# A retention layer and a gated feed-forward in one kernel: the later blocks' loads in a new order, and two small copies on another queue

## The chip, the cores and the metric

The kernel runs on one core of a Trainium2 chip. The metric is the device time of one execution in microseconds (us). The kernel before took 308.02 us (median of three runs, 307.03 to 310.31).

## The reference, cut to what matters

Eight sequences of 576 positions with eight heads of 64 features go through a retention layer: scores between a query and all earlier keys, weighted by a decay of the head, times the values. Its output, 4608 tokens of 512 features, goes through a feed-forward layer with a sigmoid gate.

```python
batch, n_heads, seq, head_dim = (8, 8, 576, 64)
n_tokens, d_model, d_ff = (4608, 512, 1536)

scores = scale * np.matmul(q, k.transpose(0, 1, 3, 2))
gamma = 1.0 - 2.0 ** (-5.0 - np.arange(H, dtype=np.float32))
Dmat = np.where(rel >= 0, gamma[:, None, None] ** rel[None, :, :], 0.0)
x = np.matmul(scores * Dmat[None, :, :, :], v)      # then heads side by side: 4608 x 512
gate = 1.0 / (1.0 + np.exp(-(x @ w_gate)))
return (gate * (x @ w_val)) @ w_out
```

## The kernel before

**Retention.** A sequence is cut into chunks of 128 positions: four whole ones and a last one of 64. Inside a chunk the kernel forms masked scores and multiplies them with the values; what comes from earlier chunks is carried in a state (the sum of key times value over the past). The first six chunks are computed in pairs during a lead-in. The other 30 (some of them made of the last halves of two sequences) are called steps, 0 to 29, and the list STEPS says which chunk each one is. The text below writes k10, q10 and v10 for the three loads of step 10.

**What a step needs before PE can use it.** `load_part(s, i)` (L164) brings k (i = 0), q (i = 1) or v (i = 2) of step s from HBM, 256 KB each, with a DMA that SP issues (L170, or L173 as two halves). `cast_qk` (L402) multiplies k and q with the decay tables and turns them to bf16, on POOL from step 2 on (L407); `cast_v` (L410) turns v to bf16, on POOL or ACT (L412). `cross(s)` (L414) then issues from SP a DMA transpose, T<-qk (L416), which turns k and q of the whole step so that features lie on partitions. Only steps 0, 1 and 7 are turned by PE instead. The scores of step s (`row`, L637) read T. The loads of the later steps go into a ring of 12 buffers, so that the load of one operand waits for the cast of the operand 12 before it.

**Feed-forward.** The tokens are taken in blocks: one of 512 in the lead-in, two of 256 and seven of 512. A block of 512 forms its products by a scheme of seven instead of eight quarter products, which costs DVE, ACT and POOL sums (`gsum` on POOL, L944 and L950, is one kind) and spares PE work. While PE computes the feed-forward of one block, the retention steps of the next are put between its products.

**What sets the order.** Nothing is scheduled by a planner; each engine runs its instructions in the order in which the program emits them. SP's queue holds in one line all loads, all transposes and the stores of the output (L916): an instruction that waits holds up everything behind it.

- In the lead-in and the two blocks of 256, `next_slot` and `next_two` (L856, L866) call `casts_to` (L823), which loads one or two steps ahead through `loads_to` (L818) and emits casts and transposes of whole steps. Slot 1 also calls `first_batch_state` (L804).
- In the blocks of 512 the list ORDER (L1087) holds twelve marks "c" a block. Each calls `next_cast` (L836) and does a third of a step: the k cast; the q cast and the transpose; or the v cast. Behind it comes one load, the same operand four steps on. The first such call, at step 10, finds the loads done up to step 11; it first catches up with `loads_to(x + 3)`, which emits all of steps 12 and 13, and then k14.

`first_batch_state` puts together the state of sequence 0 after its fourth chunk (the tile `sf`) out of four quarters of `sbd[3]`. Two of them stay on their partitions and are copied by ACT; two change from one half of the partitions to the other and go by DMA, 16 KB each, issued by SP (all four are at L809).

Of the kernel before, what the change touches and what calls it, by code (L numbers as in the profile page):

```python
# [16 lines left out]
def kernel(  # L17
# [19 lines left out]
    nc = tc.nc  # L37

    B, H, S, D = q.shape
    NT, DM = out.shape  # L40
# [71 lines left out]
    NS = len(STEPS)  # L112
# [5 lines left out]
    def pieces_of(s):  # L118

        b, c = STEPS[s]  # L120
        return [(b + j, c * P) if c == LAST else (b, c * P + j * 64) for j in range(NJ)]
# [24 lines left out]
    def half(x):  # L146
        return slice(x * 64, x * 64 + 64)

    loaded = {}
# [5 lines left out]
    def landing(shape, name, alone=False):  # L155

        tag = "ld"
        if not alone:
            early = [t for t in ("ld", "gsum") for _ in range(SLOTS[t])]
            tag = early[len(landed) % len(early)]  # L160
            landed.append(name)
        return ld_pool.tile(shape, FP32, tag=tag, name=name, bufs=SLOTS[tag])

    def load_part(s, i):  # L164

        b, c = STEPS[s]
        nm, src = (("k", k), ("q", q), ("v", v))[i]
        t = landing([P, H, D], f"{nm}32_{s}", s >= 8)
        if c < LAST:
            nc.sync.dma_start(out=t, in_=src[b, :, c * P:(c + 1) * P, :].rearrange("h p d -> p h d"))  # L170
        else:
            for j, (bj, tj) in enumerate(pieces_of(s)):
                nc.sync.dma_start(out=t[half(j)], in_=src[bj, :, tj:tj + 64, :].rearrange("h p d -> p h d"))  # L173
        loaded.setdefault(s, []).append(t)

    def load(s):
        for i in range(3):
            load_part(s, i)

    def load_pair(A):  # L180

# [220 lines left out]
    def cast_qk(s, i, eng):  # L402
        c = STEPS[s][1]
        if i == 1:
            natural_qk[s] = nat_pool.tile([P, 2, M, P], BF16, tag="qk", name=f"qk_{s}")
        tab = (qtab, ktab)[i][:, c, :].rearrange("p (y m) -> p y m", y=2).unsqueeze(3).to_broadcast([P, 2, M, D])
        eng.tensor_tensor(out=natural_qk[s][:, i].rearrange("p m (y d) -> p y m d", y=2),  # L407
                          in0=by_halves(loaded[s][1 - i]), in1=tab, op=ALU.mult)

    def cast_v(s, eng):  # L410
        natural["v", s] = nat_pool.tile([P, H, D], BF16, tag="v", name=f"v_{s}", bufs=6)
        eng(out=natural["v", s], in_=loaded[s][2])  # L412

    def cross(s):  # L414
        t = att_pool.tile([P, 2, M, P], BF16, tag="T", name=f"T_{s}", bufs=6)
        nc.sync.dma_start_transpose(out=t.rearrange("p j m t -> p (j m) t"),  # L416
                                    in_=natural_qk[s].rearrange("p j m d -> p (j m d)"))
        turned[s] = t
# [187 lines left out]
    def new_state(key, dt=BF16):  # L606
        final = dt == BF16 and key[1] == LAST - 1 and key[2] == NJ - 1
        tag = "s32" if dt == FP32 else "sf" if final else "sb"
        return nat_pool.tile([P, M, D], dt, tag=tag, name=f"{tag}_{key[0]}_{key[1]}_{key[2]}", bufs=8 if tag == "sb" else 5)
# [87 lines left out]
    def slot_of_two(vals, news):  # L697


        if vals:  # L700
# [5 lines left out]
            for j in range(NJ):  # L706
                (on_act if GLANCE_ON_ACT else on_dve)(out=glance[:, j:j + 1], in_=both[j][:, 0, 0:1])
        for s, banks in zip(news, (ROWS, ROWS_2)):
# [95 lines left out]
    def first_batch_state():  # L804

        whole = new_state((0, LAST - 1, NJ - 1))
        for hh in range(2):
            for y in range(2):
                (nc.scalar.copy if hh == y else nc.sync.dma_start)(  # L809
                    out=whole[half(y), hh::2, :], in_=sbd[3][half(hh), 2 * y:2 * y + 2, half(hh)])  # L810
        state[0, LAST - 1, NJ - 1] = whole

# [2 lines left out]
    done = {"ld": 0, "cast": 0}  # L815
    AHEAD = (1, 1, 1, 1, 1, 1, 1, 1, 1, 2, 1, 1)

    def loads_to(s):  # L818
        while done["ld"] <= min(NS - 1, s):
            load(done["ld"])  # L820
            done["ld"] += 1

    def casts_to(s):  # L823
        while done["cast"] <= min(NS - 1, s):
            x = done["cast"]
            loads_to(x + (AHEAD[x] if x < len(AHEAD) else 2))
            cast_qk(x, 1, nc.gpsimd)
            cast_qk(x, 0, nc.vector if x < 2 else nc.gpsimd)
            if x not in TURNED:
                cross(x)  # L830
            cast_v(x, on_dve if x == 0 else on_pool)
            done["cast"] += 1

    cast_part = [0]

    def next_cast():  # L836

        x = done["cast"]
        if x >= NS:
            return  # L840
        i = cast_part[0]
        if i == 0:
            loads_to(x + 3)
            cast_qk(x, 1, nc.gpsimd)
        elif i == 1:
            cast_qk(x, 0, nc.gpsimd)
            cross(x)
        else:
            cast_v(x, on_act if x >= V_ON_ACT_FROM and str(x % 4) in V_ON_ACT else on_pool)
            done["cast"] += 1  # L850
        if x + 4 < NS:
            load_part(x + 4, i)
            done["ld"] = max(done["ld"], x + 5)
        cast_part[0] = (i + 1) % 3

    def next_slot(s):  # L856
# [46 lines left out]
    def gv_tile(gvs, t0, fc):  # L903

        if fc not in gvs:
            unit = made[t0, fc // 4] = gv_unit(t0, fc // 4)
            for i in range(4):
                gvs[fc // 4 * 4 + i] = unit[:, i]
        return gvs[fc]
# [63 lines left out]
    def quarter_units(gvs, t0):  # L973
# [35 lines left out]
        def product(kind, u, i, ps, first):  # L1009
            w, x = left(kind, u, i), right(i)  # L1010
            for f in range(2):
                for kc in range(2):
                    nc.tensor.matmul(ps[:, f], lhsT=w[:, kc, f * P:(f + 1) * P], rhs=x[:, kc],  # L1013
                                     start=(first and f == 0 and kc == 0), stop=(f == 1 and kc == 1),
                                     skip_group_check=True)
# [3 lines left out]
        def quarter(kind, u, i):  # L1019

            me = of.setdefault((kind, u), {})
            if i == 1:
                gv_tile(gvs, t0, 4 * u)
                me["a"] = bank(kind, u, 0)
            if i == 5:
                me["e"] = bank(kind, u, 2)
            a, e = me.get("a"), me.get("e")
            product(kind, u, i, {1: a, 6: a, 7: a, 4: a, 5: e, 3: e, 2: me.get("g")}[i], i in (1, 5))
            settle()

            def leaves(r, h, src, eng=nc.vector):
                to = made[t0, u][:, 2 * r:2 * r + 2, h * 256:(h + 1) * 256]
                if kind == "g":
                    nc.scalar.activation(out=to, in_=src, func=AF.Sigmoid)  # L1034
                else:
                    eng.tensor_tensor(out=to, in0=to, in1=src, op=ALU.mult)  # L1036

            def finish(r, name):
                if kind + str(u) + str(r) in BY_DVE:
                    leaves(r, 1, me[name])  # L1040
                else:
                    waiting.append(lambda: leaves(r, 1, me[name], nc.gpsimd))

            if i == 1:
                me["g"] = bank(kind, u, 1)
                nc.scalar.copy(out=me["g"], in_=a)
            elif i == 2:
                leaves(0, 0, me["g"])
            elif i == 5 or i == 6:
                if i == 5:  # L1050
                    me["s5"] = keep(kind, u, "s5", e)
                me["both"] = me.get("both", 0) + 1
                if kind + str(u) not in JOINED:
                    if i == 6:
                        me["u2"] = keep(kind, u, "u2", a)
                elif me["both"] == 2:
                    nc.vector.tensor_tensor(out=e, in0=a, in1=me["s5"], op=ALU.add)  # L1057
            elif i == 3:
                if kind + str(u) in JOINED:
                    leaves(0, 1, e)  # L1060
                else:
                    nc.vector.tensor_tensor(out=me["u2"], in0=e, in1=me["u2"], op=ALU.add)  # L1062
                    finish(0, "u2")
            elif i == 7:
                nc.vector.tensor_tensor(out=me["s5"], in0=a, in1=me["s5"], op=ALU.add)  # L1065
                finish(1, "s5")
            else:
                leaves(1, 0, a)
            return 4 * 256
# [6 lines left out]
    TURN_AT = -1  # L1076
    JOINED = "g0 w0 g1 w2".split()
    BY_DVE = "w01 w00".split()
    GLANCE_ON_ACT = True
    V_ON_ACT = "2 1".split()  # L1080
    V_ON_ACT_FROM = 12
# [374 lines left out]
    step(units, 2)  # L1456
    cast_pair("q", 2, 1, nc.vector)
    step(units, 2)
    loads_to(1)
    value_sums_begin()  # L1460
    for u in range(2):
        for i in (0, 1, 3):
# [64 lines left out]
    for w, (t0, n) in enumerate(BLOCKS):  # L1527
# [3 lines left out]
        begin = slots  # L1531
# [72 lines left out]
```

## Time and profile before

| | us |
|---|---|
| median of three runs | 308.02 |
| lowest, highest | 307.03, 310.31 |
| the profiled execution | 307.51 |
| its span, first to last instruction | 305.8 |
| PE busy in it | 296.9 |
| DVE, POOL, ACT busy | 247.9, 209.0, 199.5 |

The profiled execution lies between the lowest run and the median; 1.7 us of it lie outside the span. The granted TensorE clock was 0.999. A row of a timeline gives the start, the length, engine, line, operation and operands, how many instructions were merged, and in brackets the idle time before it with what ended it. SPq and ACTq are the engines' queues that issue DMAs; their rows last as long as the issue takes, and the data lands later. A row of the waits gives the total, how often, and the longest.

### The profile page before, as it was taken

To read this page: it belongs to the slowest core of one execution; us is meant where nothing else is said; L and a number is where in the kernel's file an instruction comes from. 1 tells how busy PE (TensorE), PEld (TensorE's weight loads), DVE (VectorE), ACT (ScalarE), POOL (GpSimd) and SP (SyncE) were. 2 spreads that over 40 slices of the span, in tenths; PEclk is the share of its full clock that TensorE was granted. 3 is DMA by queue.
4 is the path that set the end of the run, shared out by engine and by line. 5 is a ranking of instruction groups with operands and counts; after the bars stand their busy time and mean duration, and the time that the engine had idled before them with its cause. 6 is when DMAs were issued, how large, how long until landed. Compare 5 with 4: busy or idle time off the path is not lost.

```text
span 305.8 us, 10631 instructions
## 1 busy us (share of the span) xinstructions
PE 296.9 (97%) x4331; PEld 240.1 (79%) x4340; DVE 247.9 (81%) x486; ACT 199.5 (65%) x455; POOL 209.0 (68%) x255
## 2 busy tenths in 40 slices
PE   7999999999999999999999999999999999999994
PEld 3664456867868887888888888888888888888883
DVE  6957986886897999689978997898789968945893
ACT  6855464645458655965796579667965896658640
POOL 5875743654477899669966996699669916751490
PEclk9999999999999999999999999999999999999999
DMA  7999998989999998997399929992890282012004
GB/s 204 338 394 399 349 283 201 238 174 158 220 205 216 253 200 168 293 192 158 44 231 231 191 42 245 194 215 56 199 183 20 70 275 74 2 59 81 3 1 139
DMA packets 144994, 55.00 MB, mean 180 GB/s; under 512 B 124336, under 2 KB 136880, under 8 KB 144944
## 3 DMA queue, kind: packets, MB, share of 16 engines
q1 hardware_dynamic: 144144, 53.66, 74.2%
q8 instruction: 34, 0.56, 0.8%
q10 hardware_dynamic: 800, 0.66, 0.7%
q14 instruction: 16, 0.13, 0.1%
HBM read 37.75 MB, written 9.44 MB: 154 GB/s over the span
## 4 chain that ended last, share of the span: by engine, by line
PE 82%; DMA 5%; DVE 4%; SPq 4%; issue 1%; POOL 1%; ACT 1%; DVEq 0%; POOLq 0%
PE gatea L1013 12%; PE wa L1013 11%; PE qa L1126 11%; PE qe L1126 8%; PE gatee L1013 6%; PE we L1013 6%; DMA T<-qk 4%; PE op L1468 3%; PE h_v L889 3%; PE h_g L889 3%; PE gateg L1013 3%; PE wg L1013 3%; PE hv L1318 3%; PE hg L1318 3%; SPq L188 3%; DMA wg<-in_moe_w_gate_dram 2%
## 5 line engine op out<-in xcount | busy, mean ns | idle before, releaser
L407 POOL TENSOR_TENSOR qk<-k,ktab 128x512 bf16<-128x512 f32 x30 | 32.4, 1080 | 19.1 <-DMA k<-in_k_dram 16.5
L1013 PEld LDWEIGHTS <-wg_sb 128*128 128x128 bf16 x336 | 32.8, 98 | 4.3
L1013 PEld LDWEIGHTS <-wv_sb 128*128 128x128 bf16 x336 | 32.9, 98 | 4.1 <-issue 0.3
L1126 PEld LDWEIGHTS <-gsum 128*128 128x128 bf16 x336 | 31.9, 98 | 5.2 <-DVE gsum L950 0.5
L950 POOL TENSOR_TENSOR gsum<-gv 128x256 bf16<-128x256 bf16 (+1 forms) x34 | 25.9, 769 | 11.7 <-DVE gv L1036 10.6
L407 POOL TENSOR_TENSOR qk<-q,qtab 128x512 bf16<-128x512 f32 x28 | 31.6, 1127 | 1.7 <-DMA q<-in_q_dram 1.7
L1013 PEld LDWEIGHTS <-wgt_sb 128*128 128x128 bf16 x252 | 24.6, 98 | 4.0 <-issue 1.2
L1013 PEld LDWEIGHTS <-wvt 128*128 128x128 bf16 x252 | 24.7, 98 | 2.9
L652 DVE TENSOR_TENSOR pt<-row,tri 128x256 bf16<-128x256 f32 x60 | 21.4, 413 | 6.7 <-PE row L645 6.7
L950 POOL TENSOR_TENSOR gsum<-gv,gsum 128x256 bf16<-128x256 bf16 x39 | 26.9, 720 | 0.0
L1036 POOL TENSOR_TENSOR gv<-gv,wu 128x512 bf16<-128x512 bf16 x7 | 8.1, 1163 | 26.4 <-DVE wu L1062 26.4
L1013 PE MATMUL wa<-xsum,wv_sb 128*128 128x256 bf16 x168 | 25.2, 273 | 0.1
L1126 PEld LDWEIGHTS <-gv 128*128 128x128 bf16 x240 | 23.0, 98 | 2.8
L1013 PE MATMUL gatea<-xsum,wg_sb 128*128 128x256 bf16 x168 | 24.1, 273 | 0.0
L613 ACT CAST sb<-s 128x256 bf16<-128x256 f32 x46 | 18.2, 415 | 4.2 <-DVE s L776 2.8
L944 POOL TENSOR_TENSOR gsum<-gv 128x256 bf16<-128x256 bf16 (+1 forms) x16 | 14.5, 909 | 7.4 <-DVE gv L1036 7.4
L1057 DVE TENSOR_TENSOR gatee<-gatea,gs 128x512 f32<-128x512 f32 x14 | 9.8, 699 | 12.0 <-PE gatea L1013 8.7
L727 ACT CAST xT<-val 128x256 bf16<-128x256 f32 x50 | 15.7, 387 | 4.2 <-PE val L679 4.2
L1036 POOL TENSOR_TENSOR gv<-gv,ws 128x512 bf16<-128x512 bf16 x14 | 16.5, 1177 | 2.6 <-DVE ws L1065 2.6
L1065 DVE TENSOR_TENSOR gs<-gatea,gs 128x512 f32<-128x512 f32 x21 | 13.8, 687 | 4.4 <-PE gatea L1013 3.6
L1065 DVE TENSOR_TENSOR ws<-wa,ws 128x512 f32<-128x512 f32 x21 | 14.4, 686 | 3.6 <-PE wa L1013 3.5
L1034 ACT ACTIVATE gv<-gs 128x512 bf16<-128x512 f32 x21 | 13.0, 630 | 6.5 <-DVE gs L1065 6.5
(182 smaller groups left out, 847.0 us busy)
## 6 DMA issues: line engine op xcount, KB each, us to landing
k<-in_k_dram SPq DMA_DIRECT2D x26, 256.0 KB, 4.2
q<-in_q_dram SPq DMA_DIRECT2D x26, 256.0 KB, 3.7
v<-in_v_dram SPq DMA_DIRECT2D x26, 256.0 KB, 4.2
out_dram<-ob SPq DMA_DIRECT2D x25, 256.0 KB, 3.0
wg<-in_moe_w_gate_dram SPq DMA_DIRECT2D x12, 256.0 KB, 5.4
wv<-in_moe_w_val_dram SPq DMA_DIRECT2D x12, 256.0 KB, 5.3
wo<-in_moe_w_out_dram SPq DMA_DIRECT2D x12, 256.0 KB, 4.8
v32p<-in_v_dram SPq DMA_DIRECT2D x6, 256.0 KB, 4.5
```

The source lines that it names most:

```text
L407: eng.tensor_tensor(out=natural_qk[s][:, i].rearrange("p m (y d) -> p y m d", y=2), in0=by_halves(loaded[s][1 - i]), in1=tab, op=ALU.mult)
L613: eng(out=state[key], in_=src)
L652: nc.vector.tensor_tensor(out=probs[s][:, y], in0=row_ps[s][y][:, 0], in1=tri.unsqueeze(1).to_broadcast([P, M, 64]), op=ALU.mult)
L727: nc.scalar.copy(out=x_out(ALL, cols_of(s, i)), in_=x_in(val_ps[s][i], cols_of(s, i)))
L889: nc.tensor.matmul(ps[:, i], lhsT=w_sb[:, kc, (fc + i) * P:(fc + i + 1) * P], rhs=xT(kc, slice(t0, t0 + n)), start=(kc == 0), stop=(kc == ...
L944: eng.tensor_tensor(out=s3, in0=a11, in1=a21, op=ALU.subtract)
L950: eng.tensor_tensor(out=to, in0=a, in1=b, op=op)
L1013: nc.tensor.matmul(ps[:, f], lhsT=w[:, kc, f * P:(f + 1) * P], rhs=x[:, kc], start=(first and f == 0 and kc == 0), stop=(f == 1 and kc == ...
L1036: eng.tensor_tensor(out=to, in0=to, in1=src, op=ALU.mult)
L1065: nc.vector.tensor_tensor(out=me["s5"], in0=a, in1=me["s5"], op=ALU.add)
L1126: nc.tensor.matmul(ps[:, b], lhsT=left(fp)[:, b * P:(b + 1) * P], rhs=right(fp), start=(first and fp == 0 and b == 0), stop=(fp == NFC // ...
L1318: nc.tensor.matmul(ps, lhsT=(wg_sb if what == "g" else wv_sb)[:, kc, fc * P:(fc + 1) * P], rhs=xT(kc, slice(0, 4 * P)), start=(kc == 0), s ...
```

## The change

Two things change in what is emitted. In `first_batch_state` the two DMAs come from ACT, between ACT's two copies. In `next_cast` the catching up is spread: `loads_to` now counts operands instead of steps, and the n-th call brings the loads to `loaded + n + n // 3`, until they are as far ahead as before (12 operands beyond the one just cast). So most calls emit one load, and each third call two. The loads now also stand behind the cast and the transpose of their call, without exception. The numbers of the calls of `loads_to` elsewhere are converted and ask for the same loads as before, and `BY_DVE_LAST` holds the same list as `BY_DVE`.

```diff
-    def load(s):
-        for i in range(3):
-            load_part(s, i)
...
-                (nc.scalar.copy if hh == y else nc.sync.dma_start)(
+                (nc.scalar.copy if hh == y else nc.scalar.dma_start)(
                     out=whole[half(y), hh::2, :], in_=sbd[3][half(hh), 2 * y:2 * y + 2, half(hh)])
...
-    def loads_to(s):
-        while done["ld"] <= min(NS - 1, s):
-            load(done["ld"])
+    def loads_to(n):
+        while done["ld"] < min(3 * NS, n):
+            load_part(*divmod(done["ld"], 3))
             done["ld"] += 1
...
-            loads_to(x + (AHEAD[x] if x < len(AHEAD) else 2))
+            loads_to(3 * (x + 1 + (AHEAD[x] if x < len(AHEAD) else 2)))
...
+        if not LOADS:
+            LOADS.update(begin=3 * x, loaded=done["ld"])
         if i == 0:
-            loads_to(x + 3)
             cast_qk(x, 1, nc.gpsimd)
...
-        if x + 4 < NS:
-            load_part(x + 4, i)
-            done["ld"] = max(done["ld"], x + 5)
+        n = 3 * x + i - LOADS["begin"] + 1
+        loads_to(min(LOADS["begin"] + n + 12, LOADS["loaded"] + n + n // 3))
         cast_part[0] = (i + 1) % 3
...
-                if kind + str(u) + str(r) in BY_DVE:
+                if kind + str(u) + str(r) in (BY_DVE if t0 + 512 < NT else BY_DVE_LAST):
...
+    BY_DVE_LAST = "w01 w00".split()
...
-    loads_to(1)
+    loads_to(6)
```

More of the change, by code (lines that the diff above doesn't have):

```diff
@@ L834 @@
     cast_part = [0]
+    LOADS = {}
     def next_cast():
```

## The prediction

> **What bounds the kernel now.** I read the page's first part, then who PE waited for, then PE's rows in order of time. The page gives the span and PE's share of it; the second fence is the head of the list of PE's waits: in total, how often, the longest.
>
> ```profile
> span 305.8 us, 10631 instructions
> PE 296.9 (97%) x4331; PEld 240.1 (79%) x4340; DVE 247.9 (81%) x486; ACT 199.5 (65%) x455; POOL 209.0 (68%) x255
> ```
>
> ```profile
> PE row L637 <- DMA T<-qk: 1.2, 2, 0.7
> ```
>
> PE is the bound: 8.9 us of the span are without a matmul, and neither part of the change removes one. Its largest wait in that list is for two transposes. PE's rows with an idle time before them, from 60 to 125 us, are these five; after 125 there is none, and what lies before 60 is emitted as it was.
>
> ```profile
> 66.83 3.40 PE L1228 MATMUL op<-wo_sb,gv 128*128 128x512 bf16 x15 [0.16 <-issue]
> 71.95 0.32 PE L637 MATMUL row<-T 64*64 64x64 bf16 x16 [0.47 <-DMA T<-qk]
> 86.39 3.40 PE L1228 MATMUL op<-wo_sb,gv 128*128 128x512 bf16 x15 [0.16 <-issue]
> 103.94 0.60 PE L1013 MATMUL gatee<-xsum,wgt_sb 128*128 128x256 bf16 x4 [0.18 <-DVE gv L1036]
> 116.61 0.32 PE L637 MATMUL row<-T 64*64 64x64 bf16 x16 [0.72 <-DMA T<-qk]
> ```
>
> They sum to 1.69 us. All that changes here is emitted inside this stretch (slot 1, and eighteen calls of `next_cast` from 92 us on), so 1.69 us is the most that it can win, 0.5%. The chain that ended last passes through the same two transposes, with the time from issue to landing:
>
> ```profile
> 66.00 5.91 DMA T<-qk
> ...
> 111.34 5.23 DMA T<-qk
> ```
>
> Counting the transposes from the first, the one at 66.00 is step 4's and the one at 111.34 is step 11's. Each has its source ready long before. These are POOL's casts of q4 and q11:
>
> ```profile
> 61.61 1.04 POOL L407 TENSOR_TENSOR qk<-q,qtab 128x512 bf16<-128x512 f32 x1
> ...
> 98.05 1.04 POOL L407 TENSOR_TENSOR qk<-q,qtab 128x512 bf16<-128x512 f32 x1 [1.50 <-DMA q<-in_q_dram]
> ```
>
> T4 could go at 61.61 + 1.04 = 62.65 and is issued 3.35 us later; T11 could go at 99.09 and is issued 12.25 us later. What held them is SP's own line.
>
> **The two copies.** SP's rows around T4:
>
> ```profile
> 61.37 1.38 SPq L809 DMA_DIRECT2D sf<-sbd  x2
> 62.85 1.38 SPq L170 DMA_DIRECT2D k<-in_k_dram  x1
> ...
> 66.00 1.63 SPq L416 DMA_TRANSPOSE T<-qk  x1
> ```
>
> Between k5 and T4 stand q5 and v5. Without the copies k5 starts at 61.37 instead of 62.85: everything behind moves up by 1.48 us. T4 then goes at 64.52, still after its source, and at 5.91 us of flight lands at 70.43. PE asked for it at 71.95 − 0.47 = 71.48, so the **0.47 us** go with 1.05 us to spare. The bounds are 0 (T4 lands no sooner) and 0.47. Whether T4 lands sooner depends on the DMA engines having room. Their share is the number before the last of these rows:
>
> ```profile
> 62.00:64.00 2.00, 2.00 (x44) 1.78 (x31) 1.94 (x5) 0.73 (x3) 1.41 (x2) 1.00 0.49 93
> 64.00:66.00 2.00, 1.95 (x10) 0.76 (x9) 1.79 (x6) 1.13 (x6) 0.00 (x0) 1.00 0.46 106
> ```
>
> They are half idle exactly while SP issues the copies and the load behind them, so I take the 0.47. The Trainium skill, page "DMA: Bandwidth & Descriptors", section "Issuing engines are not separate DMA queues", says that transfers started by different engines end on the same 16 DMA engines and interleave, so that a second issuing engine saves only the time to issue. By that rule alone, with full DMA engines, this term would be 0.
>
> On ACT the two issues come between its copies. Its rows there, and one of ACT's own issues from the start of the kernel:
>
> ```profile
> 57.25 0.60 ACT L809 COPY sf<-sbd 64x128 bf16<-64x128 bf16 x2
> 58.96 0.60 ACT L892 ACTIVATE gv<-h_g 128x512 bf16<-128x512 f32 x1 [1.11 <-PE h_g L889]
> ```
>
> ```profile
> 0.81 0.49 ACTq L188 DMA_DIRECT2D k32p<-in_k_dram  x1
> ```
>
> Two issues cost 0.98 us by ACT's row and 1.38 by SP's own row of these copies; I take 1.38, since it is the same DMA. ACT idles 1.11 us before the sigmoid at 58.96, so that sigmoid comes 0.27 us late. Behind the issues wait the second copy and this sigmoid; PE waits for the sigmoid only when it needs that bank of PSUM again. There are three such banks, and PE fills one in 0.87 us:
>
> ```profile
> 59.80 0.87 PE h_g L889 x8
> ```
>
> So two more units, 1.74 us, run before the bank is needed, and the sigmoid takes 0.60: 1.14 us of lateness are free. Cost here: **0**. The other end is an issue at its slowest on SP:
>
> ```profile
> 47.79 2.44 SPq L170 DMA_DIRECT2D q<-in_q_dram  x1
> ```
>
> Two of those, 4.88 us, less 1.11 and 1.14, would cost PE 2.6 us. Below nothing there is no gain on ACT, as it only gets work. The copies' data isn't late either way; the first reading of `sf` is at 109.8 us:
>
> ```profile
> L679 PEld LDWEIGHTS <-sf x64: 103/106/110, 109.8 to 269.8; 64*64 64x64 bf16 x64
> ```
>
> **The loads.** SP's rows from the first call of `next_cast` on, k12 to T11:
>
> ```profile
> 98.92 0.46 SPq L170 DMA_DIRECT2D k<-in_k_dram  x1
> ...
> 104.67 0.77 SPq L170 DMA_DIRECT2D k<-in_k_dram  x1
> 105.54 2.73 SPq L416 DMA_TRANSPOSE T<-qk  x1
> ...
> 111.34 1.77 SPq L416 DMA_TRANSPOSE T<-qk  x1
> ```
>
> Seven loads (k12 to k14) take 6.62 us, 0.95 each; then T10, three loads, T11. Working the new rule through by hand (36 operands loaded, n from 1): k12 | T10, q12 | v12, k13 | q13 | T11, v13 | k14, q14 | v14 | T12, k15. Ahead of T10 stands one load instead of seven, so it goes at about 99.9 instead of 105.5. Ahead of T11 stand five instead of ten: 4.7 us sooner, about 106.6, landing at about 111.9. PE asked at 116.61 − 0.72 = 115.89. The **0.72 us** go, with 4.0 us to spare; T10, read just before, is sooner still. Bounds: 0 and 0.72.
>
> What is late next? PE's product at 116.99 reads POOL's third sums (L944), and POOL has no gap there. A product of twelve matmuls takes PE 1.31 us:
>
> ```profile
> 116.26 0.71 POOL L944 TENSOR_TENSOR gsum<-gv 128x256 bf16<-128x256 bf16 x1
> 116.93 1.04 POOL L407 TENSOR_TENSOR qk<-q,qtab 128x512 bf16<-128x512 f32 x1
> ```
>
> ```profile
> 116.99 1.48 PE L1126 MATMUL qa<-wo_sb,gsum 128*128 128x256 bf16 x12
> ```
>
> ```profile
> 118.47 1.31 PE qe L1126 x12
> ```
>
> The last of these sums ends at 116.97. PE would begin that product at 116.27, but reads this sum in the ninth of twelve matmuls, 8 × 0.11 = 0.87 us in, at 117.14. It is covered by 0.17 us: tight, but the whole 0.72 stands.
>
> The price is a thinner lead. T12 waits for q12, whose cast ends at 117.97, and now k15 stands behind it, where before k15 to k16, four loads, had gone ahead of it:
>
> ```profile
> 118.00 2.15 SPq L416 DMA_TRANSPOSE T<-qk  x1
> 120.20 0.57 SPq L170 DMA_DIRECT2D q<-in_q_dram  x1
> ```
>
> ```profile
> 124.15 1.04 POOL L407 TENSOR_TENSOR qk<-k,ktab 128x512 bf16<-128x512 f32 x1
> 125.15 1.04 POOL L407 TENSOR_TENSOR qk<-q,qtab 128x512 bf16<-128x512 f32 x1
> 129.15 1.16 POOL L1036 TENSOR_TENSOR gv<-gv,wu 128x512 bf16<-128x512 bf16 x1 [2.96 <-DVE wu L1062]
> ```
>
> k15 would be issued at 120.20 and q15 at 120.8; at the median of this row, 4.2 us from issue to landing, they land at 124.4 and 125.0, against casts at 124.15 and 125.15:
>
> ```profile
> k<-in_k_dram SPq DMA_DIRECT2D x26, 256.0 KB, 4.2
> ```
>
> A lateness up to 2.96 us vanishes in POOL's wait for DVE. Between T12 and T15 then stand twelve loads (k15 to v18) instead of nine (q16 to k19); three more at 0.95 each are 2.9 us. T15 was issued at 136.03 and is read at 146.98:
>
> ```profile
> 136.03 1.87 SPq L416 DMA_TRANSPOSE T<-qk  x1
> ```
>
> ```profile
> 146.98 0.34 PE L637 MATMUL row<-T 64*64 64x64 bf16 x16
> ```
>
> At 138.9 and 5.91 us of flight it lands at 144.8. So I cost the lead at 0; its other end, should k15 or T15 take the 6 us more that would be needed to make a stage late, is the wait that T4 and T11 cause now, 0.7 us. After the eighteenth call the order is as before.
>
> **Sum.** 0.47 + 0.72 = 1.19 us. The profiled execution (307.51: 305.8 of span, 1.7 around it) becomes 306.3; it lies 0.51 under the median, so the median becomes 308.02 − 1.19 = **306.8 us**.
>
> **The rivals.**
> - The DMA engines set T4's landing, not SP. For it: T4 took 5.91 us, more than T11's 5.23, in spite of the idle before it. Against it: the share of 0.49. Only 0.72 is won: 307.3. Here the skill's rule above would be the whole story of the copies; the trace so far speaks against it.
> - POOL takes the place of T11. POOL slips by more than 0.17 us and PE waits for the third sum; the winning is 0.47 + 0.17 = 0.64: 307.4.
> - The change doesn't do what it says. The transposes' place in line isn't what delays them, SP's issues only take longer, and both waits stay: 308.0.
> - Slower: ACT is held by the two issues. From 1.11 + 1.14 = 2.25 us for both, PE waits for its bank; at the slow end this costs 2.6 us. With T4's and T11's waits gone it gives 308.02 − 1.19 + 2.6 = 309.4. For it: 2.44 us for one issue was seen on SP. Against it: that issue came behind a line of loads, and ACT's line is empty; its own rows say 0.49.
>
> **How the numbers follow.** Forecast 0.50; DMA-set T4 0.15; POOL in the way 0.10; nothing 0.11; ACT held 0.09; another gain than the two waits 0.05. Low end: 308.02 less all five idle times is 306.3, less the 0.99 by which the lowest run lies under the median: 305.3. High end: nothing won, 308.0, and half of the 2.29 by which the highest run lies over the median: 309.1. About 1%, 3.08 us, is what a measurement of this kernel can tell from no change. Faster than 304.9 is more than all idle time in the stretch: 0.04, for the spread of runs. Slower than 311.1 needs ACT held and a slow draw, or a stall I don't see: 0.07. Within: 0.89.
>
> **What would show it.** Right: PE's waits no longer name T; T4 issued near 64.5 and T11 near 106.6; ACT's sigmoid after the copies at 59.0 to 59.3; PE's product near 116 without a wait; k15 cast by 126. Wrong: a PE wait for ACT near 60 to 63, for POOL's sums near 116, or for T12 to T15 between 141 and 148, where the thinner lead would bite.

## The result

The kernel after the change takes **309.56 us** (median of 22 runs, 308.01 to 314.0) beside 307.98 for the kernel before in the same comparison (22 runs, 306.8 to 314.62). The ratio of the runs is 1.0057, 95% interval 1.004 to 1.0074: slower by 0.57%, 1.75 us of 308, where 0.4% faster was forecast. 309.56 lies outside the range of 305.3 to 309.1. Here and below the ratio is that of undisturbed runs alone, so it can differ from the quotient of the two medians. The profiled execution took 308.85 us, 1.34 more than that of before.

The first two lines of the page of after, then its list of PE's waits from 60 to 125 us (total, times, longest):

```profile
span 307.1 us, 10630 instructions
PE 297.1 (97%) x4340; PEld 239.8 (78%) x4340; DVE 249.0 (81%) x486; ACT 199.5 (65%) x455; POOL 208.2 (68%) x255
```

```profile
PE h_v L886 <- ACT gv L889: 0.9, 1, 0.9
PE val L659 <- ACT xT L744: 0.5, 1, 0.5
PE val L675 <- ACT glance L703: 0.3, 1, 0.3
```

PE's work is the same; the time without a matmul grew from 8.9 to 10.0 us (nine matmul records are missing in the profile of before, 4331 of 4340, so its 8.9 is a little too high). Neither transpose is in the list any more. In their place stand two waits for ACT, and a small third one for its `glance`, which experiments with either part show as well. PE's rows in order of time show where they lie, and one more that lies behind the stretch:

```profile
62.09 1.03 PE L886 MATMUL h_v<-xT,wv_sb 128*128 128x256 bf16 x8 [0.93 <-ACT gv L889]
63.67 0.32 PE L659 MATMUL val<-pt,v 64*64 64x64 bf16 x16 [0.54 <-ACT xT L744]
...
148.15 0.50 PE L1124 MATMUL qa<-wo_sb,gsum 128*128 128x256 bf16 x3
149.74 1.16 PE L1124 MATMUL qa<-wo_sb,gsum 128*128 128x256 bf16 x9 [1.08 <-issue]
150.73 1.47 PE L1124 MATMUL qe<-wo_sb,gsum 128*128 128x256 bf16 x12
```

Two places carry the loss. Near 62 us PE waits 0.93 + 0.54 = 1.47 us for ACT. At 148 us PE does three of the twelve matmuls of one product, stands for 1.08 us, and does the other nine; "issue" says that it waits for no engine and no transfer of data that the trace names. Such a product takes 1.31 us undisturbed. Here 150.73 − 148.15 = 2.58 us pass from its start to that of the next. In before it was 149.15 − 147.54 = 1.61:

```profile
147.54 1.77 PE L1126 MATMUL qa<-wo_sb,gsum 128*128 128x256 bf16 x12
149.15 1.47 PE L1126 MATMUL qe<-wo_sb,gsum 128*128 128x256 bf16 x12
```

So between the two profiles: −0.47 − 0.72 for the transposes, +1.47 at ACT, +0.97 at this product: +1.25 of the 1.34 us. One more standstill of PE in after is in neither sum. It lies in the lead-in, ahead of everything that changes, so it can't come from the change; smaller differences the other way make up for it:

```profile
16.99 0.21 PE L486 MATMUL st<-vp,kp 64*128 64x128 bf16 x1 [0.54 <-issue]
```

**Near 62 us: what held ACT.** ACT's rows of after:

```profile
57.50 0.73 ACTq L805 DMA_DIRECT2D sf<-sbd  x1
57.74 0.30 ACT L805 COPY sf<-sbd 64x128 bf16<-64x128 bf16 x1
60.47 0.61 ACTq L805 DMA_DIRECT2D sf<-sbd  x1
61.12 0.29 ACT L805 COPY sf<-sbd 64x128 bf16<-64x128 bf16 x1 [3.09 <-DMA k<-in_k_dram]
61.44 0.60 ACT L889 ACTIVATE gv<-h_g 128x512 bf16<-128x512 f32 x1
```

The issues are short, 0.73 and 0.61. But between the first and the second lie 2.24 us in which ACT does nothing, and the profile names as releaser a load of k, with which the copy has nothing to do. The chain of work that ended at the sigmoid passes from the load (start, time in flight) to the issue:

```profile
56.46 3.99 DMA k<-in_k_dram
60.45 0.02 issue
60.47 0.61 ACTq L805
```

The load of k4 lands at 60.45, and 0.02 us later ACT issues its copy. The program says why. Eight semaphores are handed round among all DMAs that SP and ACT issue, and an issue waits until the earlier DMA on its number has landed. That is the only wait that these four issues have; none waits for data of `sbd`. These are the copies in the program of after, on ACT, and of before, on SP:

```
ACT  L805 DMACopy sf<-sbd [waits DMAHW3_49]     (number of v3's load)
ACT  L805 DMACopy sf<-sbd [waits DMAHW5_49]     (number of k4's load)

SP   L809 DMACopy sf<-sbd [waits DMAHW1_49]     (number of k3's load)
SP   L809 DMACopy sf<-sbd [waits DMAHW2_49]     (number of q3's load)
```

On SP the numbers were those of loads that had landed long before. On ACT the second copy got that of a load just under way.

**Near 148 us: what PE stood for.** The busy share of the DMA engines is the number before the last in these rows; first before, then after:

```profile
144.00:146.00 2.00, 2.00 (x21) 1.78 (x20) 1.90 (x6) 2.00 (x8) 2.00 (x4) 1.00 0.04 8
146.00:148.00 2.00, 2.00 (x127) 1.50 (x124) 1.56 (x5) 1.78 (x6) 2.00 (x4) 1.00 0.00 0
```

```profile
144.00:146.00 2.00, 2.00 (x21) 1.79 (x19) 1.93 (x5) 1.56 (x6) 2.00 (x3) 1.00 1.07 241
146.00:148.00 2.00, 2.00 (x126) 1.72 (x127) 1.62 (x5) 1.89 (x7) 2.00 (x5) 1.00 0.90 205
```

The loads that the new rule puts off fill the DMA engines just where they were idle before. Between 146 and 148 us PE does over 120 small matmuls with as many weight loads, the densest stretch of instructions there. The list of DMA queues has one named "instruction" (packets, MB, share); the page of after:

```profile
q8 instruction: 34, 0.56, 0.7%
```

That is 16 KB a packet, and PE's 4340 matmuls and 4340 weight loads, over 34, are 255 instructions a packet: I read this queue as PE's own instruction fetch. In before, one of its packets starts between 145.5 and 145.7 us (by its own time 145.56), with the DMA engines idle. In after there is none from 145.4 to 147.4; it starts at 147.46, among loads. The queues in 147.4 to 147.6 us of after:

```profile
q1 hardware_dynamic: 172, 0.04, 94.9%
q8 instruction: 1, 0.02, 30.0%
```

PE goes on 2.28 us after that start, at 149.74. The experiments test whether this is the cause.

### The profile page after: what moved, and what is told of

It is laid out like the page before. It is cut to its first block, busy times and chain, and to the rows that moved or that the text cites. A ratio compares the mean times of both kernels' runs of the same rounds, so it can differ in the third digit from the quotient of the medians.

```text
span 307.1 us, 10630 instructions
## 1 busy us (share of the span) xinstructions
PE 297.1 (97%) x4340; PEld 239.8 (78%) x4340; DVE 249.0 (81%) x486; ACT 199.5 (65%) x455; POOL 208.2 (68%) x255
## 4 chain that ended last, share of the span: by engine, by line
PE 88%; DMA 4%; DVE 2%; ACT 2%; issue 1%; POOL 1%; SPq 0%; ACTq 0%; DVEq 0%
PE gatea L1010 12%; PE wa L1010 12%; PE qa L1124 11%; PE qe L1124 9%; PE we L1010 6%; PE gatee L1010 6%; PE op L1226 3%; PE gateg L1010 3%; PE op L1466 3%; PE wg L1010 3%; PE hv L1316 3%; PE hg L1316 3%; DMA k<-in_k_dram 3%; PE h_v L886 2%; PE h_g L886 2%; PE val L659 2%
```

## The experiments

The expectations speak of rivals for each place. For the copies: ACT is held by another DMA's landing, or only by the time that two issues take. For the loads: PE stands because its instruction fetch comes late behind data (F in the expectations), or PE is bound at this product to a time that does not move, so that whatever is won ahead of it is given back (G). Experiments 1 to 4 were compared with runs of before at 308.19 us, 5 to 8 at 308.24, 9 and 12 at 308.76.

**1. The copies alone.**

```diff
-                (nc.scalar.copy if hh == y else nc.sync.dma_start)(
+                (nc.scalar.copy if hh == y else nc.scalar.dma_start)(
```

> The two copies of sf go to ACT, the loads stay as before. Theory W (ACT's second issue waits for the landing of k4's load, whose semaphore it shares, and PE runs out of banks): PE waits 0.93 us for ACT's sigmoid and 0.54 us for ACT's xT near 62 to 64 us, T4's wait of 0.47 us is gone, T11's of 0.72 us stays: 1.0 us slower than before, 309.0. Rival (the issues themselves are slow on ACT, no wait): both ACTq rows together longer than 2.25 us. Rival (the copies are harmless and the loads cost it all): 0.5 us faster than before, 307.5.

310.03 us, ratio 1.0043 (1.0017 to 1.0069). This part alone makes the kernel slower. Experiment 10 runs it again for a profile.

**2. The loads alone.** After, with the copies on SP as before:

```diff
-                (nc.scalar.copy if hh == y else nc.scalar.dma_start)(
+                (nc.scalar.copy if hh == y else nc.sync.dma_start)(
```

> The new order of the loads, the copies stay on SP. Theory F (the loads that were put off now run at 141 to 147 us, where the trace of before has none, and hold back PE's next instructions): PE stands still for about 1.1 us near 148 us with no one to wait for; T11's 0.72 us are gone: 0.4 to 0.7 us slower than before, 308.4 to 308.7. Rival (that standstill was a chance of one execution): no standstill, 0.4 to 0.7 us faster, 307.3 to 307.6.

309.1 us, ratio 1.0023 (0.9995 to 1.0051): on the slower side, though the interval touches no change. The two parts, 0.43% and 0.23%, come to 0.66% beside 0.57% for the whole; the intervals allow that. PE's rows at the product:

```profile
148.10 0.50 PE L1124 MATMUL qa<-wo_sb,gsum 128*128 128x256 bf16 x3
150.48 1.16 PE L1124 MATMUL qa<-wo_sb,gsum 128*128 128x256 bf16 x9 [1.89 <-issue]
151.48 1.47 PE L1124 MATMUL qe<-wo_sb,gsum 128*128 128x256 bf16 x12
```

The same matmul as in after, the fourth, and a longer standstill; the fetch starts later too, at 148.29. There is no wait for ACT near 62. So the standstill belongs to the loads and the ACT waits to the copies.

**3. The copies on SP, behind step 4's transpose.** Before, with the slot's calls exchanged:

```diff
-        if s == 1:
-            first_batch_state()
         casts_to(s + LEAD_CAST)
+        if s == 1:
+            first_batch_state()
```

> The copies stay on SP but are emitted behind T4 instead of ahead of it; the loads stay as before. If SP's line alone held T4: T4 goes at 64.5 and lands near 70.4, the wait of 0.47 us goes, ACT isn't touched: 0.5 us faster than before, 307.5. If T4's landing is set by the DMA engines: T4 lands near 71.9 again, no change, 308.0. T5 stands 1.4 us behind where it stood and isn't waited for.

308.75 us, ratio 1.001 (0.9985 to 1.0035): no difference. T4's wait is gone without ACT, and yet nothing is won. PE's rows:

```profile
116.00 0.32 PE L637 MATMUL row<-T 64*64 64x64 bf16 x16 [0.29 <-DMA T<-qk]
...
146.99 0.50 PE L1126 MATMUL qa<-wo_sb,gsum 128*128 128x256 bf16 x3
147.99 1.16 PE L1126 MATMUL qa<-wo_sb,gsum 128*128 128x256 bf16 x9 [0.49 <-issue]
148.98 1.47 PE L1126 MATMUL qe<-wo_sb,gsum 128*128 128x256 bf16 x12
```

PE reaches the product 0.55 us sooner than in before and begins the next one only 0.17 us sooner. A lead of this size is lost at the product; that is what G rested on. The fetch before this product starts no sooner than in before either, at 145.64 beside 145.56.

**4. The loads given out at twice the pace, the copies on SP.** After, with

```diff
-        loads_to(min(LOADS["begin"] + n + 12, LOADS["loaded"] + n + n // 3))
+        loads_to(min(LOADS["begin"] + n + 12, LOADS["loaded"] + 2 * n))
```

and the copies as in experiment 2.

> Copies on SP. The loads catch up two at each call instead of four in three calls, so that they are as far ahead as before after six calls instead of eighteen: T10 stands behind two loads, T11 behind eight and T10. Theory F: no loads are left for 141 to 147 us, so no standstill near 148; T11 goes two loads (1.9 us) sooner than before and lands near 114.7, before PE asks at 115.9: 0.7 us faster than before, 307.3. Rival (the standstill has nothing to do with the loads): as often as in the run with the loads alone.

308.05 us, ratio 0.9989 (0.9966 to 1.0012). No transpose is waited for, and the DMA engines are idle again from 144 to 148 us. PE's rows at the product:

```profile
146.86 0.50 PE L1124 MATMUL qa<-wo_sb,gsum 128*128 128x256 bf16 x3
148.08 1.16 PE L1124 MATMUL qa<-wo_sb,gsum 128*128 128x256 bf16 x9 [0.71 <-issue]
149.07 1.47 PE L1124 MATMUL qe<-wo_sb,gsum 128*128 128x256 bf16 x12
```

The standstill is 0.71 us instead of 1.89. PE arrives 0.68 us sooner than in before; 0.60 us of it go here.

**5. Experiments 3 and 4 together.**

> Both of PE's waits for a transpose taken away without touching ACT and without leaving loads for 141 to 147 us: loads two at each call, copies on SP behind T4. If waits simply add up: 1.2 us faster than before, 307.0. Theory G (PE's own instructions come at a fixed time near 148 us, so that what PE wins earlier it waits there): PE comes to the product with its standstill about 1.1 us sooner than before, stands still 1.0 to 1.2 us in it, and starts the next product at 149.0 as before: no change, 308.0.

308.18 us, ratio 1.002 (0.9992 to 1.0047): again nothing. In its profile PE came late to the product, at 148.76, from waits in the lead-in and one of 0.73 us before 105.62 us, and began the next at 150.96, not at 149. With that G, as a fixed time, falls. What holds is the distance from the fetch's start, as the table below shows.

**6. The loads held back from the idle stretch.** The spread order, but the four that ran there come behind step 16's transpose; the copies on SP.

```diff
-        loads_to(min(LOADS["begin"] + n + 12, LOADS["loaded"] + n + n // 3))
+        ahead = LOADS["loaded"] + n + n // 3
+        if 16 <= n < 21:
+            ahead = LOADS["loaded"] + 21
+        loads_to(min(LOADS["begin"] + n + 12, ahead))
```

> The changed kernel's order of loads with the copies on SP, but k19, q19, v19 and k20 are held back behind T16, so that they are not in the DMA engines from 141 to 147 us. Theory F: the standstill shrinks from 1.9 us in the profile with the loads alone to 0.7 us or less; 0.2 to 0.5 us faster than that kernel, 308.1 to 308.4 beside 308.0 before. Rival (the loads do their harm elsewhere, in POOL's casts or in T12 to T15): as slow as with the loads alone, 0.7 us over before.

308.24 us, ratio 1.0015 (0.9986 to 1.0044). The DMA engines are idle from 144 to 148 us, the fetch starts at 145.71, and PE goes on at 148.32, after 0.92 us where 0.7 or less was expected. But a standstill of the same kind, and a longer one, appears in the next block:

```profile
148.32 1.16 PE L1127 MATMUL qa<-wo_sb,gsum 128*128 128x256 bf16 x9 [0.92 <-issue]
...
182.06 1.25 PE L1127 MATMUL qe<-wo_sb,gsum 128*128 128x256 bf16 x10 [1.64 <-issue]
```

That is where the loads now are. The DMA engines' rows of this run:

```profile
176.00:178.00 2.00, 2.00 (x97) 1.68 (x97) 1.76 (x4) 1.76 (x5) 2.00 (x4) 1.00 0.97 214
178.00:180.00 2.00, 1.94 (x64) 1.69 (x57) 1.75 (x5) 1.82 (x8) 2.00 (x4) 1.00 1.12 256
```

In before the shares there are 0.03 and 0.05, in experiment 2 they are 0.00 and 0.04, and neither has a standstill there. So the long standstill went where the loads went, from one block to the next, as F has it.

**7. More traffic in before.** The last four stores are issued once more, with the same bytes, behind the load of the nineteenth call.

```diff
+        calls[0] += 1
+        if calls[0] == 19:
+            for again in left[-4:]:
+                for at, to in zip(*again):
+                    nc.sync.dma_start(out[to, :], at)
```

> The kernel before, with its last four stores of output rows, 256 KB each, issued a second time behind k20, into the stretch from 141 us on in which its DMA engines are idle. They write the same bytes again. Theory F: PE's fetch waits behind them and PE stands still 0.9 us or more in the product near 148 us: 0.6 to 1.5 us slower than before. Rival (PE's standstill has another cause): no change, as nothing waits for these stores.

309.65 us, ratio 1.0044 (1.0015 to 1.0072), but not by F. PE waits for an output buffer that the second stores kept:

```profile
145.56 1.47 PE L1135 MATMUL qe<-wt_sb,gsum 128*128 128x256 bf16 x12 [1.11 <-ACT ob L1180]
```

The added traffic was nearly over by 144 us (a share of 1.03 up to there, 0.13 from 144 to 146 us), and the product after it took 1.49 us. This says nothing of F.

**8. The copies issued by POOL,** the loads as before.

```diff
-                (nc.scalar.copy if hh == y else nc.sync.dma_start)(
+                (nc.scalar.copy if hh == y else nc.gpsimd.dma_start)(
```

> The kernel before with the two copies issued by POOL, whose DMAs have semaphores of their own, so that no issue waits for the landing of a load. Theory W: ACT isn't held and PE's waits for ACT near 62 to 64 us don't appear; T4 goes at about 64.5; POOL has 2.4 us idle before k4's cast to take the issues. With theory G the 0.47 us of T4 are lost again near 148 us: 308.0, 1.0 us or more under the kernel with the copies alone on ACT. Rival (any second queue for the copies does the harm): as slow as that one, 309.3.

308.17 us, ratio 1.0004 (0.9984 to 1.0025). ACT isn't held, T4 isn't waited for; T11 is, for 0.78 us:

```profile
117.67 0.32 PE L637 MATMUL row<-T 64*64 64x64 bf16 x16 [0.78 <-DMA T<-qk]
```

Taking the copies off SP costs nothing, then, and gains nothing that these runs can tell; what costs is putting them on ACT.

**9. One of the two copies on ACT.** The other stays on SP; loads as before.

```diff
-                (nc.scalar.copy if hh == y else nc.sync.dma_start)(
+                (nc.scalar.copy if hh == y else (nc.scalar if hh == 0 else nc.sync).dma_start)(
```

> Only the first of the two copies goes to ACT, the other stays on SP; the loads stay as before. The copy on ACT now shares its semaphore with T2, the transpose that SP issues near 54.4 us, not with k4's load. Theory W: the issue on ACT starts when T2 lands, near 59.9 to 60.0 us, whatever ACT has done by then; ACT idles about 2 us; PE waits 0.3 to 0.6 us for ACT's sigmoid. Rival (an issue on ACT is slow by itself, or waits for the data of sbd): the issue starts right behind the copy, near 57.6 us, and PE doesn't wait for ACT.

309.67 us, ratio 1.0027 (0.9993 to 1.0061); the time alone doesn't decide, the rows do. One issue holds ACT nearly as long as two did:

```profile
57.63 0.30 ACT L809 COPY sf<-sbd 64x128 bf16<-64x128 bf16 x1
60.09 0.74 ACTq L809 DMA_DIRECT2D sf<-sbd  x1
60.87 0.29 ACT L809 COPY sf<-sbd 64x128 bf16<-64x128 bf16 x1 [2.95 <-DMA T<-qk]
```

The number handed to it is now that of T2. T2 is issued on SP at 54.53 and lands at 60.07, and ACT issues at 60.09. PE waits 0.79 and 0.54 us, more than the 0.3 to 0.6 expected. The releaser changed with the number, as only the theory of the shared semaphores has it; the time that two issues take would have halved.

**10 and 11. The copies alone and the loads alone, once more with a profile each.**

> The two copies on ACT alone, for a profile at the full clock. Theory W: ACT's second issue starts when k4 lands, near 60.5 us; PE waits 0.8 to 0.95 us for ACT's sigmoid and 0.5 us for ACT's xT; T4 lands before PE asks; T11 is still waited for, or came just in time since PE is later by 1 us.

> The loads alone, once more, for a second profile of the same program. Theory F: the DMA engines are busy from 142 to 147 us again, PE's product behind the second scores of that block takes 2.4 us or more from its start to the next product's, where 1.6 us were seen before. Rival (chance): 1.3 to 1.7 us.

312.66 and 310.61 us, one execution each, both with some 2 us lost to waits in the lead-in beside. ACT's rows and PE's of experiment 10:

```profile
61.15 2.86 ACTq L809 DMA_DIRECT2D sf<-sbd  x2
64.05 0.29 ACT L809 COPY sf<-sbd 64x128 bf16<-64x128 bf16 x1 [4.45 <-DMA sf<-sbd]
```

```profile
65.01 1.03 PE L889 MATMUL h_v<-xT,wv_sb 128*128 128x256 bf16 x8 [1.80 <-ACT gv L892]
```

Here both issues are held: v3's load lands at 61.12 and the first issue is at 61.15, k4's lands at 63.38 and the second is at 63.40. ACT idles 4.45 us and PE waits 1.80 us, then 0.55 and 0.83 more. That is about twice what was expected; the loads land later here, and ACT with them. In experiment 11 the standstill is back, at the same matmul:

```profile
148.82 0.50 PE L1124 MATMUL qa<-wo_sb,gsum 128*128 128x256 bf16 x3
150.96 1.16 PE L1124 MATMUL qa<-wo_sb,gsum 128*128 128x256 bf16 x9 [1.63 <-issue]
```

**12. Experiment 4 with the copies on POOL:** both gains, neither cost.

> The version that the runs point to: the loads two at each call, the copies issued by POOL. Both waits for a transpose go, ACT isn't held, no loads from 143 to 148 us. If the waits add up: 1.2 us faster than before, 307.0. If PE gives back most of it in the standstill near 148 us, as with the quick loads alone: 0 to 0.4 us faster.

308.32 us, ratio 0.9988 (0.9959 to 1.0018). It is not to be told from before; no version tried beats it clearly.

**The fetch and the product, over the runs** (us; start and end of the standstill from PE's rows, the fetch's start from its packet):

| kernel | DMA engines 144 to 148 | fetch starts | PE goes on | later by | PE stood | product takes |
|---|---|---|---|---|---|---|
| 12 | idle | 145.29 | 147.61 | 2.32 | 0.28 | 1.77 |
| 3 | idle | 145.64 | 147.99 | 2.35 | 0.49 | 1.99 |
| 4 | idle | 145.73 | 148.08 | 2.35 | 0.71 | 2.21 |
| 9 | idle but for its start | 147.24 | 149.59 | 2.35 | 0.83 | 2.33 |
| 6 | idle | 145.71 | 148.32 | 2.62 | 0.92 | 2.41 |
| after | busy | 147.46 | 149.74 | 2.28 | 1.08 | 2.58 |
| 11 | busy | 147.96 | 150.96 | 3.00 | 1.63 | 3.13 |
| 2 | busy in part | 148.29 | 150.48 | 2.19 | 1.89 | 3.38 |

In every profile in which PE stands here it goes on 2.2 to 3.0 us after the fetch started, wherever on the clock that is. The fetch starts 3.3 to 4.0 us after the one before it without loads (142.12 and 145.56 in before), 4.2 to 4.5 us with them (142.95 and 147.46 in after). The three profiles with loads there lose most, 2.58 to 3.38 us; those with idle engines lie at 1.49 to 2.41, also 4, 6 and 12, which keep the new rule but clear the stretch.

**What makes it more than a match of times is which matmul PE stops at.** Number PE's matmuls from 0, in the nine profiles that hold all 4340 (after, 5 to 12). From 14 us on, each standstill over 0.1 us that is put down to "issue" ends at matmul 223, 1631, 2143 or 2654. These lie 11, 4 and 4 times 128 apart (the last short by one), and 128 matmuls with their weight loads are the 16 KB of one packet. The number of packets that have started by then is 1, 12, 16 and 20: it grows in step. So PE stops at the first instructions that the packet just started brings. And of the 297 such borders in these profiles (every 128th matmul from 223 on), PE passes none sooner than 2.23 us after the start of its packet.

What the loads change is when the packet starts. Counted from PE's coming to the border before, the 16th packet starts between 0.25 us sooner and 0.86 us later in the seven of these profiles without loads there, 1.19 and 1.02 us later in after and in experiment 11. The 20th starts 2.42 us later in experiment 6, where the loads are, and at most 0.46 in the other eight. With experiment 6, where the long standstill moved with the loads, this shows F: PE waits for its own instructions, and loads in the DMA engines make them come later.

It also says what G saw. PE stands here without loads too, for 0.28 to 0.92 us in the table, when it does the 128 matmuls ahead of the border in about the time that the fetch takes (145.11 to 147.50 in experiment 3, 2.39 us, beside 2.35); the loads add to that. Why the fetch doesn't start sooner in experiments 3 and 4, although PE is ahead there, stays open. The 0.54 us at 16.99 in after are of the same kind, at matmul 223.

## Why the prediction was wrong

**PE is the bound; at most 1.69 us to win in 60 to 125 us: right,** and too narrow. Both losses are new waits, and one lies at 148 us, behind the stretch that I looked at. Two of the five idle times, 0.16 us each, weren't even idle: before's profile holds 44 matmuls of L1228 and 48 of its weight loads, and the gaps stand where a record is missing (x15 for 16). So 1.37 us was all there was.

**The copies leave SP's line: right in its mechanism.** T4 was forecast to go at 64.52 and land at 70.43; SP's row, with a landing at 69.72:

```profile
63.88 1.85 SPq L412 DMA_TRANSPOSE T<-qk  x1
```

**The 0.47 and the 0.72 us: too large.** They were waits of one execution. The copies are issued by SP in the old place in before and in experiments 2, 4, 6, 7 and 11 too, and of these six profiles only that of before shows a wait for T4 over 0.1 us. The old order of loads, with ACT not held, stands in before and in experiments 3, 7 and 8; T11 is waited for 0.72, 0.29, 0 and 0.78 us. Experiment 7, whose program is that of before up to there:

```profile
110.58 1.78 SPq L416 DMA_TRANSPOSE T<-qk  x1
...
115.86 0.32 PE L637 MATMUL row<-T 64*64 64x64 bf16 x16
```

The transpose goes 0.76 us sooner than in before, PE asks at 115.86 and finds it. On average over these profiles, 1.79 / 4 = 0.45 and 0.47 / 6 = 0.08: some 0.53 us instead of 1.19, an estimate from few profiles. And part of what is won ahead of 148 us goes at the product there, as in experiments 3 and 4.

**ACT's two issues cost 0: the step that failed.** I set their time, 1.38 us, against 2.25 us of slack. The time was right: 0.73 + 0.61 = 1.34. What I left out is that a DMA's issue can wait, and for whom: for the landing of another DMA on the same semaphore. That wait, 2.24 us, came on top, and PE paid 1.47. The change adds a wait to ACT, and I didn't ask for what. The rival "ACT is held by the two issues", with a chance of 0.09 and 309.4 us, came nearest to the time and named the waits for ACT, but its mechanism, a slow issue behind a full line, is not the one seen. The Trainium skill, page "DMA: Bandwidth & Descriptors", section "Issuing engines are not separate DMA queues", says that starting DMAs from several engines saves only the time to initiate them. Here it saved that on SP, 1.38 us, and cost ACT more: 3.09 us idle.

**The loads: the forecast places were conservative, the mechanism right.** T10 and T11 were forecast at about 99.9 and 106.6:

```profile
97.30 2.93 SPq L412 DMA_TRANSPOSE T<-qk  x1
103.55 2.45 SPq L412 DMA_TRANSPOSE T<-qk  x1
```

**POOL's third sum covers by 0.17 us: not tried in after,** where PE comes to that product at 117.65, later than in before. In experiment 12 it comes at 116.26, as early as forecast; POOL's sum ends at 116.46 there, and PE doesn't wait for it.

**The thinner lead costs 0: right for what I named, wrong as a sum.** k15 was cast at 125.21, and POOL still waits 2.61 us for DVE behind:

```profile
129.86 1.17 POOL L1033 TENSOR_TENSOR gv<-gv,wu 128x512 bf16<-128x512 bf16 x1 [2.61 <-DVE wu L1059]
```

No transpose is late. But I followed the put-off loads only to those who read them, not to who else uses the DMA engines while they move. The sum has no term for the 0.97 us at 148: that is the second step that failed.

So the forecast missed two costs, 1.47 and 0.97 us, and overrated the gains of 1.19. By the profiles of after and before the change costs +1.25 us; with the gains at their average it is 1.47 + 0.97 − 0.53 = 1.9 us. The 1.75 us measured lie between the two.

## What to carry to other kernels

Before a DMA is moved to a compute engine, read in the program which semaphore its issue waits on and which transfer had that number last: the engine stands until that transfer has landed, however short the issue. When transfers are put off into a stretch where the DMA engines were idle, ask what used that idleness, PE's instruction fetch in a stretch of many small matmuls above all. A wait of half a microsecond in one profile is not yet a gain: see whether it stands in a second one of the same program.

## What the runs showed of the hardware

- In this program an engine that issues a DMA waits for an unrelated transfer on the same semaphore, to within 0.03 us: k4's landing at 60.45 and the issue at 60.47 in after, T2's at 60.07 and 60.09 in experiment 9, v3's at 61.12 and 61.15 and k4's at 63.38 and 63.40 in experiment 10.
- A queue named "instruction" moves 16 KB packets, which the profile counts among those of the 16 DMA engines. Each brings 128 matmuls with their weight loads, and PE never came to the first of them sooner than 2.23 us after its packet started (297 cases). Among loads one packet started 4.5 us after its forerunner (after), with idle engines 3.4 us (before), and the standstill of PE at that product came to 1.08 to 1.89 us with loads, to 0.92 us at most without. The Trainium skill, page "Runtime: NRT & Kernel Launch", section "Instruction fetch mechanics", says that the fetch comes in blocks of 16 KiB through a DMA queue of the sequencer and that its cost is mostly hidden. The packets agree with it: 0.56 MB in 34. With loads in the DMA engines the cost was not hidden.
